# Product with v in float32: two heads in column halves, one broadcast per half later on, and an order planned with other durations

## The chip, the cores and the metric

One core of one Trainium2 chip. The metric is the device time of one execution in microseconds (us). The engines are TensorE (PE, with its weight loads shown apart as PEld), VectorE (DVE), ScalarE (ACT), GpSimd (POOL) and SyncE (SP), which issues most DMAs.

## The reference, cut to what matters

```python
def _attn_ref(q, k, v, g_norm):            # 8 batches, 8 heads, 576 x 64: linear attention
    kv = np.einsum('bhsd,bhse->bhde', k, v)
    out = np.einsum('bhsd,bhde->bhse', q, kv)
    rms = np.sqrt(np.mean(out * out, axis=-1, keepdims=True) + 1e-06)
    return (out / rms * g_norm).astype(np.float32)
...
def _moe_ref(x, w_gate, wq, wk, wv, wo):   # x: 8 x 576 x 512, 4 experts, the top 2 kept
    ...
    for e in range(E):
        q = x @ wq[e]
        k = x @ wk[e]
        v = x @ wv[e]
        scores = scale * (q @ k.transpose(0, 2, 1))
        scores = np.where(causal, -1000000000.0, scores)
        ...                                # softmax over the last axis: a
        ye = a @ v @ wo[e]
        ...                                # added where e is in the top 2, times its weight
def _moe2_ref(x, w_in, g_ln, w_sg, b_sg, w_out):
    h = gelu(x @ w_in)                     # 512 -> 1024, cut into u and v
    v_n = layer_norm(v) * g_ln
    v_s = np.einsum('ts,bsd->btd', w_sg, v_n) + b_sg[None, :, None]
    return x + (u * v_s) @ w_out
```

## The kernel before, in words

The work has two phases. Phase 1 goes over the 8 batches: `front` (k times v, q times that, the sum of squares), `normall` (the RMS scale), `qkpart` and `vpart` (projections for the four experts, called heads here), and `attn` (causal attention of the four heads, in five row blocks each: 128, 128, 128, 96, 96 rows). `conversions` splits the later weights into two parts in between. Phase 2 is the gated MLP, whose products the trace calls `ps`.

Most products run in the one-pass type float32r. To keep float32 accuracy an operand is split into a high part and the rest (`hi` and `lo`, or `h` and `l` at the end of a name), and the products of the parts are added up in PSUM. A product in plain float32 stands in the trace as two MATMUL rows per instruction of the program: `kvps` (k times v), `outps` (`outT`, q times that), `statps` (`stat`, four 32-column tiles side by side, marked by `together`) and `wxps`.

For a head e, `scores` makes the scores (`scps`), their masked minimum (DVE, into `prob` and `small`) and the exponential (ACT). `transp` transposes a row block on PE (`tps`), copies it as float32r into `aTh` (ACT), and writes the rest, `tps` minus `aTh`, into `aTl` (DVE). `av` multiplies with v: the tile `vst` holds, per head, 64 columns of v's high part and 64 of its rest, so a product gives both in 128 PSUM partitions (`avps`). It runs 7 pairs of products per head (over `aTh`, then `aTl`), with 256, 128, 320, 320, 320, 192 and 96 columns. ACT copies one half of `avps` to `avt`, DVE adds the other into `gav`. After the second head of a pair, the gate weights `R` are transposed (`rps`) and multiplied in, and `gav` is split and written to DRAM for phase 2.

`norm` broadcasts the scale `rr` over the partitions by a product with `bsel_sb`, into the tile `nps`, for two halves of 288 columns in each of 4 column groups. The loop `for _ in range(2)` issues that product twice.

The order on each engine is not that of the code. Every call is first recorded as an `Op`; `merge` interleaves the generators by the windows in `OPT["w"]` (in batches; `u` is the first part of phase 2), and `Recorder.plan` then plays the recorded operations through a model of the chip: `cost` gives each a duration, `LAG` the signalling time, `RATE` the DMA rate, `Clock` the TensorE clock. An engine takes the earliest recorded operation that is ready by the model and whose tiles are free. `trace` emits the program in that order, so the queue of each engine is fixed. Every instruction of it has the line of the call in `trace`, L440; the tile names tell them apart. Attention tiles in PSUM (`scps`, `tps`, `avps`, `rps`) share four banks, the other phase 1 tiles three, `statps` has one.

Of the kernel before, what the change touches and what calls it, by code (L numbers as in the profile page):

```python
# [48 lines left out]
OPT = dict(ob=1, sx=0, pinq=0, dv=0, pin=1, cvb=2, xb=1, ldb=2, hp={}, n1=0, n2=0, f1=0, pa=4, sA=(), dg=0, cost=(1.01, 0.88, 1.22, 1.47, 1.28), avi=1, prb=4, ahb=2, alb=2, qkb=2, ahead=3, w={'attn': (0.206, 1.26), 'qk1': (0.056, 0.272), 'qk0': (-0.534, -0.135), 'v': (-0.716, -0.324), 'front': (-1.368, -0.958), 'norm': (-0.947, -0.848), 'conv': (-0.324, 3.644), 'conv2': (3.213, 7.228), 'wts': (-1.719, -1.149), 'u': (0.212, 1.281), 'front_0': (-1.763, -1.646), 'v_0': (-1.24, -0.97), 'qk0_0': (-1.252, -1.036), 'qk1_0': (-0.092, 0.063), 'norm_0': (-1.641, -1.541)})  # L49
# [21 lines left out]
LAG = {"tensor": 0.25, "vector": 0.15, "scalar": 0.15, "gpsimd": 0.15, "sync": 0.6, "dma": 0.4}  # L71
RATE = 220e3
# [92 lines left out]
class Op:  # L165
    __slots__ = ("eng", "fn", "args", "kw", "tiles", "pred", "succ", "need", "n", "idx", "dur", "ready", "start", "done", "work", "group")
# [65 lines left out]
class Recorder:  # L232
# [16 lines left out]
    def together(self, ops):  # L249
        first = ops[0]  # L250
        for op in ops:
            op.group = ops
            first.pred.update(o for o in op.pred if o not in ops)
            first.need += [t for t in op.need if t not in first.need]

    def add(self, eng, fn, args, kw):
# [39 lines left out]
        op.dur = self.cost(op, outs, ins)  # L296
        if eng == "tensor":
            passes = 2 if fn == "transpose" else 4 if ins[0].dtype == F32 else 1
            op.work = min(op.dur, op.n * passes / 2400.0)
# [3 lines left out]
    def cost(self, op, outs, ins):  # L303

        n, fn = op.n, op.fn
        if op.eng == "tensor":
            if fn == "transpose":
                return 0.110
            if ins[0].dtype == F32 and len(outs[0].part) == 32:
                return n / 2400.0  # L310
            if ins[0].dtype == F32:
                return max(n * 4 / 2400.0, 0.22)
            return max(n / 2400.0 + 0.0125, 0.11)
        if op.eng == "vector":
            if fn == "memset":
                return 0.15
            extra = {"scalar_tensor_tensor": 0.06, "tensor_tensor_reduce": 0.09, "reciprocal": 0.05}.get(fn, 0.0)
            return 0.155 + 0.00103 * n + extra
        if op.eng == "scalar":
            return 0.155 + 0.00089 * n + (0.33 if "accum_out" in op.kw else 0.0) if fn != "preload_act_table_set" else 1.3  # L320
        if op.eng == "gpsimd":
            return 0.7 if fn == "dma_start" else max(0.5, 0.12 + 0.0023 * n)
        return 0.5

    def plan(self, margin=LAG):
# [30 lines left out]
        now, chain = 0.0, []  # L356
        while events:
# [11 lines left out]
            for e in self.ENGINES:  # L369
# [3 lines left out]
                for k, (_, op) in enumerate(row):  # L373
# [12 lines left out]
                    free_at[e] = now + op.dur  # L386
                    if e == "tensor":
                        free_at[e] += op.dur * sum([c.half(now) for c in clocks]) / len(clocks)
                        for c in clocks:
                            c.add(now, free_at[e], op.work)  # L390
                    push(free_at[e], "free", None)
                    end = free_at[e]
                    if op.fn == "dma_start":
                        size = self.size(op)
                        pipe = max(pipe, end) + size / RATE
                        end = pipe + 1.8
                    elif e == "tensor":
                        end += 0.1
                    op.done = end
                    push(end + 0.05, "gone", op)  # L400
                    for s in op.succ:
                        lag = 0.05 if s.eng == e and op.fn != "dma_start" else margin[s.eng]
                        if op.fn == "dma_start":
                            lag += margin["dma"]
                        if s.eng == e == "tensor":
                            lag = -0.1
                        s.ready = max(s.ready, end + lag)
# [41 lines left out]
class Phase1:  # L449
# [31 lines left out]
    def first_loads(self):  # L481

        nc = self.nc
        more = self.vv.tile([P, 2, 2, NQ, P], F32, name="kvmore", tag="vst")
# [14 lines left out]
    def staging(self, n):  # L499
        k = len(self.stg)  # L500
        return self.at.tile([P, n], F32, name="wstage", tag=f"aT{'hl'[k // 2]}1", bufs=2)
# [144 lines left out]
    def qk_half(self, st, pr, is_k, h):  # L646
        nc = self.nc
        col = 256 * is_k + P * pr
# [34 lines left out]
    def vproj(self, st, s):  # L683
        nc = self.nc
        m = _rows(s)
# [12 lines left out]
        nc.scalar.copy(vst[:m, s, :, 0:64], src)  # L698
        nc.vector.tensor_tensor(vst[:m, s, :, 64:128], src, vst[:m, s, :, 0:64].bitcast(F32), op=OP.subtract)
# [54 lines left out]
    def vpart(self, b, st):  # L754
        nc = self.nc
        st["qs"], st["kh"], st["kl"] = [], [], []
        st["vst"] = self.vv.tile([P, NQ, E, P], F32R, name="vst", tag="vst")
# [64 lines left out]
    def transp(self, st, e, i):  # L822
# [4 lines left out]
        if i == 0:  # L827
            st["aT"][e] = tuple(
                (
                    self.at.tile([P, 2, 256], F32R, name=f"aT{n}0", tag=f"aT{n}0", bufs=bf),  # L830
                    self.at.tile([P, NQ, 320], F32R, name=f"aT{n}1", tag=f"aT{n}1", bufs=bf),
                )
                for n, bf in (("h", OPT["ahb"]), ("l", OPT["alb"]))
            )
        hi, lo = st["aT"][e]
        ps = self.bank("tps", True)
        full = min(i + 1, 4)
        for j in range(i + 1):
# [3 lines left out]
        jobs = [  # L842
            (ps[:, 0 : full * m].rearrange("p (j f) -> p j f", j=full), lambda t: t[n][:, 0:full, q : q + m])
        ]
        if i == 4:
            jobs.append((ps[:96, 4 * m : 5 * m], lambda t: t[1][:96, 4, q : q + m]))
# [5 lines left out]
    def av(self, b, st, e):  # L852
        nc = self.nc
        parts = st["aT"].pop(e)
        vst = st["vst"]
        if e % 2 == 0:
            st["gav"] = self.at.tile([P, S], F32, name="gav", tag="gav", bufs=1)
        gav = st["gav"]
        dst = gav[0:64] if e % 2 == 0 else gav[64:128]
        t = self.at.tile([P, S], F32, name="avt", tag="avt", bufs=2)  # L860
        for n, (c0, c1, js) in enumerate(((0, 256, 2), (256, S, NQ))):
            ps = self.bank("avps", True)[:, 0 : c1 - c0]
            for j in range(js):
                kr = _rows(j)
                q0 = max(c0, _first(j))
                for x, a in enumerate(parts):
                    nc.tensor.matmul(
                        ps[:, q0 - c0 :],
                        vst[:kr, j, e, :],
                        a[n][:kr, j, q0 - c0 : c1 - c0],  # L870
                        start=(j == 0 and x == 0),
                        stop=(j == js - 1 and x == 1),
                    )
            nc.scalar.copy(t[64:128, c0:c1], ps[0:64])
            nc.vector.tensor_tensor(dst[:, c0:c1], ps[64:128], t[64:128, c0:c1], op=OP.add)
        if e % 2:
            R = st["R"][e // 2]
# [558 lines left out]
```

## Time and profile before

| | |
|---|---|
| median of 3 runs | 855.81 us (855.45 to 856.19) |
| profiled execution | 858.0 us, of which the span from first to last instruction is 856.2 us |
| granted TensorE clock | 0.992 of full, mean of the span |
| PE busy | 826.9 us (97%) |
| DVE, ACT, POOL busy | 526.0, 449.6, 321.9 us |

A matmul's busy time includes the time until its result is out, in which the next one already runs, so busy times of PE overlap. What a product takes of PE's time is the distance from its start to the start of the next one.

### The profile page before, as it was taken

What the parts mean: (1) busy time and instruction counts of PE and PEld (TensorE: products, weight loads), DVE (VectorE), ACT (ScalarE), POOL (GpSimd) and SP (SyncE); (2) the same over time, 40 slices, a digit from 0 to 9 for tenths busy, and PEclk for the clock granted to TensorE, in tenths of its full rate; (3) what the DMA queues carried; (4) which work ended last, traced back from release to release, by engine and by line L of the source; (5) the groups of instructions that cost most, each with busy time, mean ns of one, the idle gap of its engine ahead of it and who ended that gap; (6) DMA issues with size and microseconds to landing.
All of it is one profiled execution on the core that took longest, in us unless ns stands there. A gap on an engine that the chain in (4) does not pass through costs nothing.

```text
span 856.2 us, 16001 instructions
## 1 busy us (share of the span) xinstructions
PE 826.9 (97%) x5552; PEld 754.4 (88%) x5552; DVE 526.0 (61%) x1450; ACT 449.6 (53%) x1200; POOL 321.9 (38%) x387
## 2 busy tenths in 40 slices
PE   6599999999999999999998899999999999999998
PEld 5497999999899999998996789898989889898996
DVE  1657777887776776978886788453444435340330
ACT  2546566776766677676876794432333233321110
POOL 0872733854633253564651155231213222220120
PEclk9699999999999999999999999999999999999999
DMA  9576583874856768664549680111202030101011
GB/s 302 168 208 153 146 229 113 238 206 126 252 155 188 201 157 239 185 187 135 148 131 278 204 289 10 59 47 46 85 25 81 25 105 13 38 13 50 13 38 61
DMA packets 77090, 114.44 MB, mean 134 GB/s; under 512 B 13265, under 2 KB 40593, under 8 KB 77010
## 3 DMA queue, kind: packets, MB, share of 16 engines
q1 hardware_dynamic: 76866, 112.90, 45.1%
q8 instruction: 44, 0.72, 0.4%
q0 software_dynamic: 144, 0.52, 0.2%
q14 instruction: 36, 0.29, 0.1%
HBM read 58.31 MB, written 26.77 MB: 99 GB/s over the span
## 4 chain that ended last, share of the span: by engine, by line
PE 86%; DVE 5%; DMA 5%; ACT 1%; POOL 1%; issue 1%; SPq 1%; DVEq 0%; ACTq 0%
PE ps L440 42%; PE qkps L440 10%; PE scps L440 6%; PE vps L440 6%; PE avps L440 5%; PE tps L440 5%; PE kvps L440 3%; PE outps L440 3%; PE nps L440 2%; PE wxps L440 2%; DMA cv_w<-in_w_in 1%; DVE o L440 1%; DMA wstage<-in_wqkvg 1%; PE statps L440 1%; DMA kvmore<-in_kvp 1%; PE rps L440 1%
## 5 line engine op out<-in xcount | busy, mean ns | idle before, releaser
L440 PE MATMUL ps<-wsh,vn 128*128 128x288 f32 x576 | 120.2, 295 | 0.0
L440 ACT ACTIVATE prob<-prob,small 128x128 f32<-128x128 f32 (+4 forms) x160 | 96.8, 605 | 17.9 <-DVE small L440 16.3
L440 PEld LDWEIGHTS ps<-wsh,vn 128*128 128x128 f32 x576 | 94.3, 188 | 0.9 <-DVE g L440 0.3
L440 POOL TENSOR_TENSOR gl<-g,gh 128x512 fp32r<-128x512 f32 x32 | 41.6, 1300 | 135.5 <-ACT gh L440 135.4
L440 DVE CUSTOM_DVE_ANT_0 prob<-scps,mask_sb 128x128 f32<-128x128 f32 (+4 forms) x160 | 75.9, 478 | 25.9 <-PE scps L440 23.9
L440 DVE TENSOR_TENSOR aTl<-tps,aTh 128x384 fp32r<-128x384 f32 (+1 forms) x192 | 79.7, 432 | 6.2 <-ACT aTh L440 5.4
L440 PE MATMUL qkps<-xhi,whi 128*128 128x288 f32 x256 | 78.7, 307 | 0.0
L440 ACT CAST aTh<-tps 128x384 fp32r<-128x384 f32 (+1 forms) x192 | 69.1, 381 | 16.5 <-PE tps L440 14.4
L440 PE MATMUL qkps<-xhi,wlo 128*128 128x288 f32 x256 | 77.0, 301 | 0.0
L440 PE MATMUL qkps<-xlo,whi 128*128 128x288 f32 x256 | 77.0, 301 | 0.0
L440 PE MATMUL ps<-wsl,vn 128*128 128x288 f32 x256 | 75.5, 295 | 0.0
L440 PE MATMUL tps<-id_sb,prob 96*128 96x96 f32 (+2 forms) x480 | 71.7, 258 | 0.8 <-DVE small L440 0.4
L440 PE MATMUL scps<-kh,qs 128*128 128x128 f32 (+2 forms) x192 | 68.6, 361 | 2.0 <-DVE gav L440 0.6
L440 POOL TENSOR_SCALAR lny<-mv 128x1 f32<-128x1 f32 x36 | 24.3, 676 | 119.3 <-DVE mv L440 119.0
L440 ACT CAST gh<-g 128x512 fp32r<-128x512 f32 x32 | 19.9, 620 | 80.4 <-DVE g L440 62.8
L440 POOL TENSOR_TENSOR xlo<-o,xhi 128x576 fp32r<-128x576 f32 (+1 forms) x32 | 42.8, 1362 | 51.3 <-ACT xhi L440 51.2
L440 PE MATMUL avps<-aTh,vst 128*128 128x320 f32 (+4 forms) x224 | 59.0, 286 | 2.7 <-DVE gav L440 1.8
L440 DVE TENSOR_TENSOR g<-ps,u 128x288 f32<-128x288 f32 x64 | 28.9, 453 | 52.7 <-PE ps L440 52.7
L440 PE MATMUL scps<-kl,qs 128*128 128x128 f32 (+2 forms) x192 | 59.8, 315 | 0.4 <-DMA kl<-loT 0.4
L440 PEld LDWEIGHTS tps<-id_sb,prob 96*128 96x128 f32 (+2 forms) x480 | 52.8, 139 | 7.7 <-issue 2.8
L440 PE MATMUL avps<-aTl,vst 128*128 128x320 f32 (+4 forms) x224 | 56.4, 290 | 0.0
L440 ACT ACTIVATE vn<-vg,lny 128x512 fp32r<-128x512 f32 x32 | 22.9, 723 | 54.8 <-POOL lny L440 53.4
(177 smaller groups left out, 2431.7 us busy)
## 6 DMA issues: line engine op xcount, KB each, us to landing
kv<-in_kvp SPq DMA_DIRECT2D x30, 384.0 KB, 4.9
kh<-hiT SPq DMA_DIRECT2D x64, 144.0 KB, 3.0
kl<-loT SPq DMA_DIRECT2D x64, 144.0 KB, 3.1
q<-in_qT SPq DMA_DIRECT2D x30, 288.0 KB, 4.7
out<-oev SPq DMA_DIRECT2D x32, 256.0 KB, 2.0
kv<-in_kvp SPq DMA_DIRECT2D x30, 192.0 KB, 4.9
qs<-hiT SPq DMA_DIRECT2D x32, 144.0 KB, 2.6
qs<-loT SPq DMA_DIRECT2D x32, 144.0 KB, 2.6
```

The lines of the kernel that those rows point to most:

```text
L440: f(*[val(v) for v in op.args], **{k: val(v) for k, v in op.kw.items()})
```

## The change

The product with v takes plain float32: `aT` is one copy of the transposed block, in float32, made by ACT or DVE in turn; `vst` holds v once, 64 columns per head, also copied by ACT or DVE in turn. `av` now handles a pair of heads at once. The first head's 64 output rows go to PSUM partitions 0 to 63, the second's to 64 to 127, and the 14 products of the pair (28 MATMUL rows in the trace) are kept together in the order. One ACT copy per PSUM bank fills `gav`. In batches 1 to 7 the broadcast in `norm` is issued once. The planner's durations, lags and rate are other numbers, with a time for a change of tile size; the windows are other numbers as well. Three assertions state that the weights are recorded before use. The tile for two early loads no longer shares the buffers of `vst`.

```diff
@@ the windows (OPT) and the planner's numbers
-..., avi=1, prb=4, ahb=2, ..., w={'attn': (0.206, 1.26), ..., 'u': (0.212, 1.281), ...})
+..., avi=1, prb=4, ahb=4, ..., w={'attn': (0.177, 1.304), ..., 'u': (-0.111, 1.169), ...})
-LAG = {"tensor": 0.25, "vector": 0.15, "scalar": 0.15, "gpsimd": 0.15, "sync": 0.6, "dma": 0.4}
-RATE = 220e3
+LAG = {"tensor": 0.12, "vector": 0.13, "scalar": 0.13, "gpsimd": 0.13, "sync": 0.25, "dma": 0.12}
+MODE = 0.15
+RATE = 230e3
@@ def norm
-            for _ in range(2):
+            for _ in range(1 if b else 2):
                 nc.tensor.matmul(ps, self.bsel_sb[:, c, h, :], self.rr, start=True, stop=True)
@@ def vproj
-        nc.scalar.copy(vst[:m, s, :, 0:64], src)
-        nc.vector.tensor_tensor(vst[:m, s, :, 64:128], src, vst[:m, s, :, 0:64].bitcast(F32), op=OP.subtract)
+        (nc.scalar.copy if s % 2 else nc.vector.tensor_copy)(vst[:m, s], src)
@@ def transp
         for src, dst in jobs:
-            nc.scalar.copy(dst(hi), src)
-        for src, dst in jobs:
-            nc.vector.tensor_tensor(dst(lo), src, dst(hi).bitcast(F32), op=OP.subtract)
+            (nc.scalar.copy if (e + i) % 2 else nc.vector.tensor_copy)(dst, src)
@@ def av
+        for n, (c0, c1, js) in enumerate(parts2):
+            ps = banks[n]
             for j in range(js):
                 kr = _rows(j)
+                q0 = max(c0, _first(j)) - c0
+                ops += [
                     nc.tensor.matmul(
-                        ps[:, q0 - c0 :],
-                        vst[:kr, j, e, :],
-                        a[n][:kr, j, q0 - c0 : c1 - c0],
+                        ps[64 * h : 64 * h + 64, q0:],
+                        vst[:kr, j, 2 * pr + h, :],
+                        parts[h][n][:kr, j, q0 : c1 - c0],
...
+                    for h in range(2)
+                ]
+        nc.together(ops)
+        for ps, (c0, c1, _) in zip(banks, parts2):
+            nc.scalar.copy(gav[:, c0:c1], ps)
@@ def attn
-                if i == OPT["avi"] and e > 0:
-                    with self.hp("a"):
-                        self.av(b, st, e - 1)
-                    yield 1.0
-        self.av(b, st, E - 1)
-        yield 1.0
+                if i == OPT["avi"] and e == 2:
+                    self.av(b, st, 0)
+                    yield 2.0
+        self.av(b, st, 1)
+        yield 2.0
```

Three places of the order on PE follow. The first is the broadcast of batch 1, PE before (`kh`, `kl`, `qs` are the split k and q of batch 0's attention, which goes on meanwhile):

```order
L440 MATMUL nps<-rr,bsel_sb 128x288 x2
L440 MATMUL scps<-kh_576,qs_463 96x288
L440 MATMUL scps<-kl_587,qs_463 96x288
L440 MATMUL nps<-rr,bsel_sb 128x288 x2
L440 MATMUL scps<-kh_576,qs_463 96x288
L440 MATMUL scps<-kl_587,qs_463 96x288
```

PE now, at the same place:

```order
L453 MATMUL nps<-rr,bsel_sb 128x288
L453 MATMUL tps<-id_sb,prob 128x128
L453 MATMUL scps<-kh_564,qs_473 96x288
L453 MATMUL scps<-kl_572,qs_473 96x288
L453 MATMUL nps<-rr,bsel_sb 128x288
L453 MATMUL scps<-kh_564,qs_473 96x288
L453 MATMUL scps<-kl_572,qs_473 96x288
```

One broadcast per half stands where two stood; other products still lie between two halves.

The second place is the product with v of a head in the last batch, PE before, and ahead of it the transposes that fill the next head's tile:

```order
L440 MATMUL tps<-id_sb,prob 128x128 x2
L440 MATMUL avps<-aTh_7215,vst 128x256
L440 MATMUL avps<-aTl_7222,vst 128x256
L440 MATMUL avps<-aTh_7215,vst 128x128
L440 MATMUL avps<-aTl_7222,vst 128x128
L440 MATMUL avps<-aTh_7266,vst 128x320
L440 MATMUL avps<-aTl_7275,vst 128x320
```

PE now, the first pair of batch 1, with what stands ahead of it:

```order
L453 MATMUL tps<-id_sb,prob 128x128 x2
L453 MATMUL qkps<-xhi,whi 128x288
L453 MATMUL qkps<-xlo,whi 128x288
L453 MATMUL qkps<-xhi,wlo 128x288
L453 MATMUL qkps<-xhi,whi 128x288
L453 MATMUL qkps<-xlo,whi 128x288
L453 MATMUL qkps<-xhi,wlo 128x288
L453 MATMUL avps<-aT_1685,vst 64x256
L453 MATMUL avps<-aT_1830,vst 64x256
L453 MATMUL avps<-aT_1685,vst 64x128
L453 MATMUL avps<-aT_1830,vst 64x128
```

The two heads' tiles alternate, and 64 rows of output stand where 128 stood. In 13 of the 16 pairs projections (`qkps`, at times with two broadcasts behind them) stand in this way between the last transposes and the block, in the last pair seven of phase 2's first products; in the last pair of batch 6 and the first of batch 7 it is a few scores at most.

The third place is where phase 2 joins the last batch's attention, PE before. Between the last projection of batch 7 and the first `ps` row stand 28 `scps`, 26 `tps`, 28 `avps` and 5 `rps` products and nothing else:

```order
L440 MATMUL scps<-kh_7129,qs_7057 128x256
L440 MATMUL scps<-kl_7144,qs_7057 128x256
L440 MATMUL ps_7386<-wih_7280,xh 128x512
L440 MATMUL ps_7392<-wih_7280,xh 128x512
L440 MATMUL ps_7395<-wih_7280,xh 128x512
L440 MATMUL ps_7400<-wih_7280,xh 128x512
L440 MATMUL tps<-id_sb,prob 128x96 x4
```

PE now; between the last projection and the first `ps` row stand 34 `scps`, 38 `tps`, 28 `avps` (two pairs) and 5 `rps`:

```order
L453 MATMUL avps<-aT_6565,vst 64x96
L453 MATMUL avps<-aT_6678,vst 64x96
L453 MATMUL ps_6764<-wih_6643,xh 128x512
L453 MATMUL ps_6769<-wih_6643,xh 128x512
L453 MATMUL ps_6772<-wih_6643,xh 128x512
L453 MATMUL ps_6774<-wih_6643,xh 128x512
L453 MATMUL rps<-id_sb,R 128x128 x3
```

Behind the last scores and ahead of the first product that needs normalized rows (`ps<-wsh,vn`), 28 `ps` products of 512 columns now stand where 6 stood, and 60 of 288 columns in both.

## Rows read from the trace of the kernel before

**Rows 1.** The page: span, and busy time of each engine over the span.

```profile
span 856.2 us, 16001 instructions
PE 826.9 (97%) x5552; PEld 754.4 (88%) x5552; DVE 526.0 (61%) x1450; ACT 449.6 (53%) x1200; POOL 321.9 (38%) x387
```

**Rows 2.** Windows: from:to, length, busy per engine, granted clock, DMA share, GB/s.

```profile
0.00:50.00 50.00, 33.51 (x186) 29.23 (x187) 21.89 (x55) 19.58 (x53) 26.03 (x43) 0.86 0.74 224
50.00:400.00 350.00, 348.30 (x2675) 326.08 (x2673) 270.95 (x888) 245.18 (x722) 171.97 (x200) 1.00 0.67 186
400.00:447.00 47.00, 46.33 (x355) 44.12 (x355) 41.85 (x137) 33.95 (x102) 25.59 (x32) 1.00 0.48 131
447.00:500.00 53.00, 46.39 (x292) 37.97 (x290) 41.14 (x120) 39.14 (x102) 13.87 (x18) 1.00 0.71 222
500.00:856.00 356.00, 352.39 (x2053) 317.06 (x2051) 150.17 (x255) 111.71 (x226) 84.47 (x98) 1.00 0.17 57
```

**Rows 3.** Waits of PE, whole span: us in total, times, longest.

```profile
PE nps L440 <- DVE rr L440: 9.3, 1, 9.3
PE kvps L440 <- DMA kv<-in_kvp: 4.7, 2, 4.4
```

**Rows 4.** Timeline of PE, one head's product with v: start, us, what.

```profile
315.63 0.28 PE L440 MATMUL avps<-aTh,vst 128*128 128x256 f32 x1
...
317.18 0.23 PE L440 MATMUL avps<-aTh,vst 96*128 96x96 f32 x1
317.24 0.28 PE L440 MATMUL avps<-aTl,vst 96*128 96x96 f32 x1
317.35 0.32 PE L440 MATMUL vps<-whi,xhi 128*96 128x260 f32 x1
```

**Rows 5.** Timeline of PE around the four-tile float32 product of batch 3.

```profile
173.23 0.30 PE L440 MATMUL qkps<-xhi,whi 128*128 128x288 f32 x1
173.37 0.29 PE L440 MATMUL qkps<-xlo,whi 128*128 128x288 f32 x1
173.59 1.18 PE L440 MATMUL statps<-sq,sel_sb 128*32 128x288 f32 x16
174.70 0.44 PE L440 MATMUL tps<-id_sb,prob 128*128 128x128 f32 x2
```

**Rows 6.** The chain that ended last, a float32 product across the whole array: start, us.

```profile
65.52 0.97 PE outps L440 x4
```

**Rows 7.** Timeline of PE, broadcasts of a later batch.

```profile
294.53 0.44 PE L440 MATMUL nps<-rr,bsel_sb 128*128 128x288 f32 x2
294.80 0.28 PE L440 MATMUL avps<-aTl,vst 128*128 128x256 f32 x1
...
295.36 1.66 PE L440 MATMUL nps<-rr,bsel_sb 128*128 128x288 f32 x8
296.92 0.40 PE L440 MATMUL qkps<-xhi,whi 128*128 128x288 f32 x1
```

**Rows 8.** Groups on DVE and ACT: count, busy us, mean ns, idle before them.

```profile
L440 DVE TENSOR_TENSOR aTl<-tps,aTh 128x384 fp32r<-128x384 f32 (+1 forms) x192 | 79.7, 432 | 6.2 <-ACT aTh L440 5.4
...
L440 ACT CAST aTh<-tps 128x384 fp32r<-128x384 f32 (+1 forms) x192 | 69.1, 381 | 16.5 <-PE tps L440 14.4 <-DVE aTl L440 0.8
...
L440 DVE TENSOR_TENSOR gav<-avps,avt 64x256 f32<-64x256 f32 x64 | 29.1, 460 | 5.7 <-ACT avt L440 3.9
...
L440 ACT COPY avt<-avps 64x256 f32<-64x256 f32 x64 | 24.9, 392 | 8.7 <-PE avps L440 7.7
...
L440 DVE TENSOR_TENSOR vst<-vps,vst 128x256 fp32r<-128x256 f32 (+1 forms) x40 | 16.4, 415 | 0.7 <-ACT vst L440 0.7
```

**Rows 9.** The chain that ended last, where phase 2 begins: start, us, what.

```profile
447.45 0.57 DVE aTl L440
...
458.24 5.30 DMA xl<-gvl
...
486.95 1.25 ACT aTh L440 x3
488.20 0.04 issue
488.24 1.17 DVE aTl L440 x3
```

More of the change, by code (lines that the diff above doesn't have):

```diff
@@ L165 @@
 class Op:
-    __slots__ = ("eng", "fn", "args", "kw", "tiles", "pred", "succ", "need", "n", "idx", "dur", "ready", "start", "done", "work", "group")
+    __slots__ = ("eng", "fn", "args", "kw", "tiles", "pred", "succ", "need", "n", "idx", "dur", "ready", "start", "done", "work", "group", "lat", "load", "mode")
     def __init__(self, eng, fn, args, kw):
@@ L249, in together @@
     def together(self, ops):
-        first = ops[0]
+        first, tiles = ops[0], P // ops[0].mode[1]
         for op in ops:
-            op.group = ops
+            op.group, op.dur, op.load, op.work = ops, op.dur / tiles, op.load / tiles, op.work / tiles
+            op.lat = op.dur + 0.17
             first.pred.update(o for o in op.pred if o not in ops)
@@ L354, in can @@
             return True
-        now, chain = 0.0, []
+        now, chain, mode, last = 0.0, [], (P, P), 0.0
         while events:
@@ L385, in plan @@
                     op.start = now
-                    free_at[e] = now + op.dur
                     if e == "tensor":
-                        free_at[e] += op.dur * sum([c.half(now) for c in clocks]) / len(clocks)
-                        for c in clocks:
-                            c.add(now, free_at[e], op.work)
+                        half = sum([c.half(now) for c in clocks]) / len(clocks)
+                        turn = MODE if op.mode != mode else 0.0
+                        begin = max(now + turn, (now + turn if turn else last) + op.load)
@@ L391, in plan @@
+                        mode, last = op.mode, begin
+                        free_at[e] = begin + op.dur * (1 + half)
+                        for c in clocks:
+                            c.add(begin, free_at[e], op.work)
+                        end = free_at[e] + op.lat - op.dur
+                    else:
+                        free_at[e] = now + op.dur
+                        end = now + op.lat
                     push(free_at[e], "free", None)
-                    end = free_at[e]
                     if op.fn == "dma_start":
[L394 to L398, printed above, removed]
+                        pipe = max(pipe, end) + self.size(op) / RATE
+                        end = pipe + 1.7
@@ L483, in first_loads @@
         nc = self.nc
-        more = self.vv.tile([P, 2, 2, NQ, P], F32, name="kvmore", tag="vst")
+        more = self.at.tile([P, 2, 2, NQ, P], F32, name="kvmore", tag="more", bufs=1)
         for n in range(NC):
@@ L500, in staging @@
         k = len(self.stg)
[L501 removed]
+        return self.at.tile([P, n], F32, name="wstage", tag="aT1", bufs=OPT["ahb"])
     def load(self, n, kv=None, q=None):
@@ L827, in transp @@
         if i == 0:
[L828 to L835, printed above, removed]
+            st["aT"][e] = [
+                self.at.tile([P, 2, 256], F32, name="aT0", tag="aT0", bufs=OPT["ahb"]),
+                self.at.tile([P, NQ, 320], F32, name="aT1", tag="aT1", bufs=OPT["ahb"]),
+            ]
+        aT = st["aT"][e]
         ps = self.bank("tps", True)
@@ L849, in transp, with av @@
-        for src, dst in jobs:
-            nc.vector.tensor_tensor(dst(lo), src, dst(hi).bitcast(F32), op=OP.subtract)
-    def av(self, b, st, e):
+            (nc.scalar.copy if (e + i) % 2 else nc.vector.tensor_copy)(dst, src)
+    def av(self, b, st, pr):
         nc = self.nc
[L854 to L862, printed above, removed]
+        parts = [st["aT"].pop(2 * pr + h) for h in range(2)]
+        vst, R = st["vst"], st["R"][pr]
+        gav = self.at.tile([P, S], F32, name="gav", tag="gav", bufs=1)
+        parts2 = ((0, 256, 2), (256, S, NQ))
+        banks = [self.bank("avps", True)[:, 0 : c1 - c0] for c0, c1, _ in parts2]
+        ops = []
+        for n, (c0, c1, js) in enumerate(parts2):
+            ps = banks[n]
@@ L892, in attn @@
+        hi = self.at.tile([P, S], F32R, name="gvh", tag="gvh", bufs=1)
+        lo = self.at.tile([P, S], F32R, name="gvl", tag="gvl", bufs=1)
+        nc.scalar.copy(hi, gav)
+        nc.gpsimd.tensor_tensor(lo, gav, hi.bitcast(F32), op=OP.subtract)
+        for t, dst in zip((hi, lo), self.gvd[b]):
+            nc.sync.dma_start(dst[pr].bitcast(F32), t.bitcast(F32))
     def attn(self, b, st):
```

98 lines of the change are left out of this document (48 added, 50 removed).

## The prediction

> **What bounds the kernel now.** I read the page first: PE is busy for 826.9 of 856.2 us, DVE for 526.0, ACT for 449.6 [rows 1]. Then the windows, to see where that average hides something. From 50 to 400 us PE is busy for 348.3 of 350 us, from 500 on for 352.4 of 356, and the granted clock is 1.00 [rows 2]. In these stretches PE is the limit, and every microsecond of its work that goes shortens the span, unless something new becomes late. Two stretches differ. In the first 50 us PE is busy for 33.5 us; the waits name one of 9.3 us for `rr` and two for loads [rows 3]. From 447 to 500 us, where the last batch's attention has no projections left beside it and phase 2 begins, PE is busy for 46.4 of 53 us. That understates the gap, since busy times overlap. Weight loads show it better: in the dense stretch they are busy for 326.08/350 = 0.93 of the time, here for 37.97 us, which at 0.93 is 40.8 us of dense work, so some 12 us are lost (10.4 us by the density of 500 to 856 us, 0.89) [rows 2]. DVE is busy for 41.1 and ACT for 39.1 of the 53 us, and the chain runs from `aTh` on ACT to `aTl` on DVE and only then to the product with v [rows 2, 9].
>
> **The broadcast.** Seven batches times four groups times two halves are 56 products of 288 columns that go. Two adjacent ones with another product behind them take 0.27 us from start to start, 0.135 each, as the 0.14 of a projection of the same width [rows 5, 7]. So 56 x 0.135 = 7.6 us, in stretches where PE never rests. Bounds: eight in a row took 1.56 us to the next product, 0.195 each [rows 7], which gives 10.9 us. At the other end, that pace is set by who reads the banks, and then the second issue costs little: if PE had to wait for DVE anyway, 0. The new order puts scores and transposes between the halves in batch 1 and two broadcasts ahead of a block of 2.98 us (below) elsewhere, so DVE's reading is covered; I take 7.5.
>
> **The product with v.** A head's block now takes 317.35 - 315.63 = 1.72 us, 14 rows [rows 4]; 32 blocks are 55.0 us. The new block has, per head, 256 + 128 + 3 x 320 + 192 + 96 = 1632 columns in float32. What float32 costs on the whole array is seen at `outps`: four rows, two products of 288 columns, take 0.97 us, so 0.485 each or 1.68 ns per column [rows 6]. One head alone would take 1632 x 1.68 = 2.75 us, more than the 1.72 of two float32r passes. The change lives on two heads running side by side. No row of before has tiles of 64 columns, but `statps` has four of 32: 16 rows, eight float32 products of 288 columns. One after another these would take 8 x 0.485 = 3.88 us; the next product starts 1.11 us behind the first, where four abreast give 0.97. The remaining 0.14 us, and the 0.22 - 0.13 = 0.09 us longer step from the projection into the block, are the price of going to the other tile size and back [rows 5]. So a pair takes 2.75 + 0.23 = 2.98 us, sixteen take 47.7 us, and 7.3 us go.
>
> Weights: each half loads 64 columns per pass. The 96-column product whose next weights are not ready yet takes 0.11 us where its neighbour takes 0.06 [rows 4]; if 128 columns of load cost 0.11 us and the two halves load in turn, only the 96-column step (0.08 us a pass at 0.84 ns) is short, by 0.03 us twice a pair: 1 us in all. Not abreast at all, a pair takes 2 x 2.75 + 0.23 = 5.73 us, sixteen 91.7 us: 36.7 us more than now. I take the gain of 7.3, since the nearest row shows four abreast without loss.
>
> A block must not wait for the last copy of its second head. In 13 pairs six or more projections (0.8 us at 0.13) lie between the last transposes and the block, in the last pair phase 2's products; a copy takes 0.38 to 0.43 us [rows 8]. Two pairs have little cover: at most about 0.5 us each, 1 us.
>
> **Copies.** DVE loses `aTl` (79.7 us), the `gav` sums (29.1) and the rest of v (16.4), and gains 96 of the copies that ACT made at 0.38 us and 24 copies of v at 0.42 or less: -125 + 37 + 10 = -78 us. ACT loses half of its 69.1 us of `aTh`, and `avt` (24.9), and gains 32 copies of `gav` at about 0.39: some -47 us, more with the copies of v that it gives up [rows 8]. Beside a full PE this is worth nothing; that work was hidden. It counts where PE waits, from 447 to 500 us: there the two-step `aTh` then `aTl` becomes one step, and DVE, some 78% busy, loses about a fifth of the 376 us that it works up to 500 us [rows 2]. Also, 28 wide products of phase 2 instead of 6 now stand behind the last scores, 22 x 0.23 = 5 us of work that lies beside the first normalizations (0.23 is 512 columns at 0.13/288 a column). Against it, the stretch ahead has three heads without filler where it had two and some. Bounds: 0, and the whole 10 to 12 us. I take half, 6 us; the load of `xl` (5.3 us in the chain [rows 9]) and the normalization stay.
>
> **The rest.** The first 50 us keep both issues, the loads come in nearly the same order and `rr` hangs on the same steps of DVE and ACT: 0, with 1.5 us either way. The planner's new numbers move rows within a stretch; between 50 and 400 and after 500 us an order can't make PE's work shorter, so 0 there, with a loss of up to 5 us if shorter lags place a product ahead of its data.
>
> **Sum.** 7.5 + 7.3 + 6 = 20.8 us from the span's 856.2 give 835.4. The profiled execution took 858.0 us, 1.8 more than its span, and the median of the runs (855.81) lies 0.4 us below that span; I let that stand: 835 us.
>
> **The rivals.** *The halves run one after the other* (slower). Then the product with v costs 36.7 more instead of 7.3 less: 855.8 + 36.7 - 7.5 - 6 = 879 us. It decides once the pair takes more than (55.0 + 13.5)/16 = 4.28 us, that is once less than about half of one head's time is hidden behind the other. For it: no 64-column tile is seen, and the weights are twice as wide as those of `statps`. Against it: the row of four abreast. 4%.
>
> *Partly abreast.* Two streams and two weight loads get in each other's way, and the pair takes 3.2 to 4.2 us: with 3.7 us it is 59.2 us, 4.2 more than now, and the time is 846 to 847. For it speaks only the width. The Trainium skill's page "TensorE: Matmul & The Clock Gate", "Measured speedup vs the span model", gives three column tiles a speedup of 2.38; two at that efficiency would make 1.59 instead of 2 (an estimate from that page), 5.5/1.59 + 0.23 = 3.7 us a pair and the same 846 us. No row here shows such a loss: `statps` reaches 3.88/1.11 = 3.5 of 4 with the change of mode included. 7%.
>
> *The work goes but waits take its place.* The order was planned with shorter lags; products come to the head of PE's queue before their data, and 447 to 500 us stays as it is: 14.8 us less work, 3 to 12 us of new waits, 844 to 853 us. For it: PE's queue can't pass a late product. Against it: the middle has long runs of projections as cover. 8%; and 2% that such waits exceed 17 us, so slower.
>
> *The broadcasts and blocks were not the limit* (the change does not do what it says): another engine paces 50 to 400 us, and the time stays within 0.2% (1.7 us; I call less no change). PE busy for 348 of 350 us speaks against it. 2%.
>
> *All of the tail comes back, and the broadcasts are worth their upper bound*: 855.8 - 10.9 - 7.3 - 12 = 825.6, so 824 to 828 us. 4%.
>
> **How the numbers follow.** The forecast, 835 us with a range of its own from 828 to 843, has 73%; with the cases above this is 100%. 827 to 848 us leaves out the serial halves (4%), the slower waits and the unchanged case (4%), the top half of the other waits (4%) and half of the best case (2%), 14%. Faster: 73 + 7 + 8 + 4 = 92%; same 2%; slower 4 + 2 = 6%.
>
> **What would show it.** Right: `avps` has 448 rows, in sets of two that start within some 0.02 us; a pair takes 2.9 to 3.1 us from its first row to the next product; `nps` has 72 rows; DVE's busy time falls to about 450 us and ACT's to about 400; the weight-load density from the last projection to the solid `ps` run rises and that stretch shortens by some 6 us; phase 2's solid run stays at about 336 to 356 us. Wrong: the second half of a set starts 0.2 to 0.5 us behind the first; waits of PE for `aT` at the head of the blocks or a granted clock under 1.00 in the middle; or the long wait for `rr` grown past 11 us.

## The result, and the profile after

The changed kernel takes 847.24 us (median of 4 runs, 846.26 to 848.11), the kernel before 855.80 beside it: a ratio of 0.990 (95% interval 0.9882 to 0.9917). It is faster, by 8.6 us, where 20.8 were forecast; the time lies inside the range, near its upper end. The page of the profiled execution (847.4 us, to be read beside [rows 1]):

```profile
span 845.6 us, 15457 instructions
PE 811.3 (96%) x5496; PEld 722.2 (85%) x5496; DVE 462.3 (55%) x1274; ACT 398.0 (47%) x1048; POOL 321.9 (38%) x387
```

PE lost 15.6 us of busy time, DVE 64 and ACT 52; the prediction had 400 us for ACT and 450 for DVE, which is busy for 12 us more than that. The windows, with the columns of [rows 2] (the fourth row is the tail, as the fourth of [rows 2], some 10 us earlier):

```profile
0.00:50.00 50.00, 33.94 (x172) 28.02 (x173) 21.51 (x54) 19.04 (x52) 28.39 (x45) 0.83 0.75 224
50.00:400.00 350.00, 343.27 (x2682) 306.56 (x2681) 237.36 (x785) 213.48 (x629) 188.19 (x219) 1.00 0.70 191
400.00:437.00 37.00, 37.00 (x304) 35.12 (x303) 24.08 (x95) 22.23 (x65) 10.01 (x12) 1.00 0.49 129
437.00:488.00 51.00, 43.27 (x283) 34.04 (x282) 32.54 (x95) 31.50 (x79) 15.15 (x19) 0.93 0.67 209
488.00:845.00 357.00, 353.78 (x2065) 318.44 (x2064) 146.85 (x248) 111.80 (x226) 80.11 (x93) 1.00 0.17 59
```

Between 50 and 400 us PE was busy for 348.30 of 350; now it is for 343.27. And in the tail the mean granted clock is 0.93, where it was 1.00. The waits of PE, whole span (us in total, times, longest), say where:

```profile
PE outps L453 <- DVE bd L453: 7.9, 3, 6.6
PE ps L453 <- ACT vg L453: 6.8, 1, 6.8
PE kvps L453 <- DMA kv<-in_kvp: 4.1, 1, 4.1
PE tps L453 <- ACT aT L453: 2.6, 4, 0.7
PE scps L453 <- DVE aT L453: 2.1, 3, 0.9
```

The first is the idle time ahead of `rr` under another name [rows 3]: `outps` of batch 1 now stands ahead of the broadcast. The second, 6.8 us in one piece, is new. The last two are new too: six of these seven waits end 1.8 to 2.4 us behind the start of a long `ya`, of which more below.

The product with v itself does what was forecast. PE around the first pair of batch 1:

```profile
103.51 0.29 PE L453 MATMUL qkps<-xhi,whi 128*128 128x288 f32 x1
103.73 2.98 PE L453 MATMUL avps<-aT,vst 128*64 128x256 f32 x28
106.64 0.45 PE L453 MATMUL statps<-sq,sel_sb 128*32 128x288 f32 x4
```

From the first row of the block to the next product it is 106.64 - 103.73 = 2.91 us, and 2.91 in 15 of the 16 pairs (2.98 forecast; two heads took 2 x 1.72 = 3.44 [rows 4]). The second row of a set starts 6 to 7 ns behind the first.

Where PE's time went, worked out from the timelines of PE as the distance from each product's start to the next one's, summed by the tile it writes (us; a wait counts to the product ahead of it). The last three columns are experiments:

| tile | before | after | `a_late` | `a_mid` | `a_best` |
|---|---|---|---|---|---|
| `avps` | 57.2 | 46.9 | 46.5 | 46.9 | 46.7 |
| `nps` | 23.7 | 18.2 | 18.2 | 19.4 | 19.4 |
| `scps`, `tps` | 116.0 | 112.0 | 111.9 | 108.7 | 108.6 |
| `qkps`, `vps` | 169.6 | 173.7 | 173.7 | 171.8 | 172.5 |
| `ps` | 371.7 | 379.2 | 371.9 | 379.3 | 372.6 |
| the others | 109.4 | 107.3 | 107.3 | 107.2 | 106.1 |
| sum | 847.7 | 837.3 | 829.5 | 833.2 | 825.8 |

The two products that the change is about lost 10.3 + 5.5 = 15.8 us; 14.8 were forecast. All else was to lose 6 more, and gained 5.5.

### The profile page after: what moved, and what is told of

The parts are those of the page before. It is cut to its first block, busy times and chain, and to the rows that moved or that the text cites. A ratio compares the mean times of both kernels' runs of the same rounds, so it can differ in the third digit from the quotient of the medians.

```text
span 845.6 us, 15457 instructions
## 1 busy us (share of the span) xinstructions
PE 811.3 (96%) x5496; PEld 722.2 (85%) x5496; DVE 462.3 (55%) x1274; ACT 398.0 (47%) x1048; POOL 321.9 (38%) x387
## 4 chain that ended last, share of the span: by engine, by line
PE 84%; DVE 7%; POOL 3%; ACT 3%; issue 2%; DMA 1%; SPq 0%; ACTq 0%; POOLq 0%; DVEq 0%
PE ps L453 42%; PE qkps L453 10%; PE vps L453 7%; PE scps L453 5%; PE tps L453 4%; PE avps L453 4%; PE kvps L453 4%; PE outps L453 4%; PE wxps L453 2%; PE nps L453 1%; DVE ya L453 1%; DVE yb L453 1%; DVE prob L453 1%; DMA q<-in_qT 1%; PE statps L453 1%
## 5 line engine op out<-in xcount | busy, mean ns | idle before, releaser
L453 DVE CUSTOM_DVE_ANT_0 prob<-scps,mask_sb 128x128 f32<-128x128 f32 (+4 forms) x160 | 73.8, 474 | 6.1 <-PE scps L453 5.3
L453 PEld LDWEIGHTS qkps<-xhi,whi 128*128 128x128 f32 x256 | 48.7, 190 | 2.4 <-issue 1.7
L453 PE MATMUL ps<-wo2h,gl 128*128 128x512 f32 x128 | 50.1, 391 | 0.0
L453 PE MATMUL ps<-wo2l,gh 128*128 128x512 f32 x128 | 50.0, 391 | 0.0
L453 PE MATMUL ps<-wo2h,gh 128*128 128x512 f32 x128 | 49.9, 390 | 0.0
L453 PEld LDWEIGHTS qkps<-xlo,whi 128*128 128x128 f32 x256 | 48.9, 191 | 0.4
```

Of the source, the lines that this page charges most:

```text
L453: f(*[val(v) for v in op.args], **{k: val(v) for k, v in op.kw.items()})
```

## Two places in the trace where the rest was lost

**The tail.** PE, ACT and the windows (columns of [rows 2]) around the wait of 6.8 us:

```profile
475.86 0.29 PE L453 MATMUL ps<-xl,wih 128*128 128x288 f32 x1
482.95 0.61 PE L453 MATMUL ps<-xh,wih 128*128 128x288 f32 x1 [6.80 <-ACT vg L453]
483.35 0.44 PE L453 MATMUL ps<-xl,wih 128*128 128x288 f32 x1
```

```profile
476.77 0.63 ACT L453 ACTIVATE vg<-vraw 128x512 f32<-128x512 f32 x1 [0.65 <-DVE vn L453]
480.70 0.72 ACT L453 ACTIVATE vn<-vg,lny 128x512 fp32r<-128x512 f32 x1 [3.30 <-POOL lny L453]
482.30 0.60 ACT L453 ACTIVATE vg<-ps 128x512 f32<-128x512 f32 x1 [0.88 <-DVE vn L453]
```

```profile
476.00:480.40 4.40, 0.15 (x2) 0.00 (x0) 3.81 (x7) 0.76 (x2) 2.33 (x4) 1.00 0.00 0
480.40:483.00 2.60, 0.05 (x1) 0.05 (x1) 0.82 (x2) 1.42 (x3) 0.26 (x1) 0.50 0.00 0
483.00:487.20 4.20, 4.15 (x16) 3.80 (x17) 2.23 (x5) 1.54 (x3) 2.65 (x3) 0.50 0.18 70
```

The 512-column products that make v of phase 2 hold a PSUM bank until ACT's Gelu (`vg`) has read it. Phase 2's first part (`ps1`) has four banks. The Gelu stands in ACT's queue behind `vn`, which waits for POOL's `lny`, and a `vg` buffer is free only after DVE's `vn`. So the next 288-column product, which needs no normalized row at all, finds no bank for 7 us. The granted clock, full (2.4 GHz) since 43.5 us, falls to its lower level (1.2 GHz) from 480.4 to 487.2 us, in this idle time. The products from 482.95 to 487.2 take 0.24 us each in place of 0.13, another 2 us.

**The middle.** The four engines around one of the waits in batch 3's attention:

```profile
222.20 1.42 POOL L453 TENSOR_TENSOR gvl<-gav,gvh 128x576 fp32r<-128x576 f32 x1 [5.32 <-ACT gvh L453]
```

```profile
222.41 1.53 DVE L453 SCALAR_TENSOR_TENSOR ya<-yb,ya 128x288 f32<-128x288 f32 x1
```

```profile
223.97 0.43 ACT L453 CAST yh<-ya 128x288 fp32r<-128x288 f32 x1 [0.95 <-DVE ya L453]
224.31 0.47 ACT L453 COPY aT<-tps 128x384 f32<-128x384 f32 x1
```

```profile
224.84 0.63 PE L453 MATMUL tps<-id_sb,prob 96*128 96x96 f32 x5 [0.75 <-ACT aT L453]
```

`ya` is a step of the RMS scale of the next batch. It starts 0.2 us behind POOL's `gvl` and ends 0.3 us behind its end. ACT's `yh` waits for it, a copy `aT` stands behind `yh`, and PE waits for the bank that this copy frees. How often that happens shows in the rows of the tile `ya` (ns, least, median, most), before and after:

```profile
L440 DVE SCALAR_TENSOR_TENSOR ya<-yb,ya x8: 452/460/861, 30.9 to 397.4; 128x288 f32<-128x288 f32 x8
```

```profile
L453 DVE SCALAR_TENSOR_TENSOR ya<-yb,ya x8: 459/1397/1531, 28.8 to 385.0; 128x288 f32<-128x288 f32 x8
...
L453 DVE SCALAR_TENSOR_TENSOR o<-o,g_sb,nps x64: 500/508/517, 31.9 to 401.7; 128x288 f32<-128x288 f32 x64
```

In the new order `ya` stands beside `gvl` in six of seven later batches, before in none. The last row is the control: `o` has the same form, but reads one operand from PSUM, and is never longer than 0.517 us, though 40 of the 64 run beside a POOL operation for 0.2 us or more. The Trainium skill's page "SBUF — State Buffer", "SBUF: two separate sides" (with its part "Who interferes with whom"), says that a DVE operation with two inputs in SBUF and a GpSimd operation that reads SBUF exclude each other for the whole instruction, and that one with at most one SBUF input does not contend, unless it runs in a mode that uses two ports. This trace agrees for these two, 1.40 against 0.46 us for `ya` and 0.51 throughout for `o`. One SBUF tensor is no assurance, though: `yc`, `ya` times a factor per partition, takes 0.36 us as a rule, and 1.06 and 1.32 us in the two batches of the experiment `a_mid` (below) where it runs beside `gvl`; which mode it runs in, no row shows.

```profile
L460 DVE TENSOR_SCALAR yc<-ya,side x8: 354/362/1318, 30.6 to 380.8; 128x288 f32<-128x288 f32 x8
```

## The experiments

They ran on other chips than the first comparison, on which the kernel before took 856.3 to 857.4 us; so ratios to it are compared (the changed kernel: 0.990). "In its own order" means that the planner saw the unchanged program, and only the emission differs.

**Broadcasts twice again, `a_twice`.**

```diff
-            f(*[val(v) for v in op.args], **{k: val(v) for k, v in op.kw.items()})
+            for _ in range(op.alt or 1):        # alt = 2 for nps of batches 1 to 7
+                f(*[val(v) for v in op.args], **{k: val(v) for k, v in op.kw.items()})
```

> The changed kernel in its own order, with every broadcast of batches 1 to 7 issued twice in a row again; nothing else moves. If the broadcasts were full work of PE, as the forecast has it, 56 x 0.135 = 7.5 us come back: 847.2 + 7.5 = 854.8 us. If PE had spare time around them in the new order (it now waits some 7 us in the middle), less comes back: 847 to 851 us.

853.17 us, 0.9956 (0.9942 to 0.9971). The difference from 0.990 is 0.0056, 4.8 us, and 5.5 us by the spans (851.1 and 845.6). On the timeline `nps` takes 25.6 us in place of 18.2, the full 7.4, and the stretch in which these broadcasts stand, from the first scores to the last projection, is 6.1 us longer. So in the new order the broadcast is real work, worth 4.8 to 6.1 us where 7.5 were forecast.

**Once in the old order, `b_once`, and in batches 2 to 6 only, `b_once26`.** The second product is left out when the program is emitted, in the order of before.

> The kernel before in its own order, with the second of the two broadcasts left out in batches 1 to 7; nothing else moves. By the forecast's price 56 x 0.135 = 7.5 us go: a ratio of 0.991, about 848.3 us. If some of the broadcasts stood where PE would have waited for DVE's reading anyway, less: 850 to 855.

856.31 us, 0.9989 (0.9974 to 1.0005): no difference that can be measured, and by the interval a gain of at most 2.2 us. In the old order the price was not there. How long PE's weight loads waited ahead of the broadcasts for DVE's `o`, which reads the bank of `nps`, in the kernel before and in this run (us, times, longest):

```profile
PEld nps L440 <- DVE o L440: 1.6, 5, 0.6
PEld nps L442 <- DVE o L442: 3.8, 14, 0.6
```

A bank of `nps` becomes free when DVE has read it. In batches 1 to 7 a single broadcast now takes 0.24 us to the next product (median), where a pair took 0.33, so `nps` loses 3.9 us on the timeline (23.7 to 19.8) and not 7.5. Windows around the broadcasts of batch 1, columns of [rows 2]:

```profile
74.00:80.00 6.00, 5.41 (x31) 4.04 (x31) 5.62 (x17) 4.81 (x13) 2.10 (x2) 1.00 0.46 111
80.00:82.00 2.00, 1.15 (x8) 0.75 (x8) 1.94 (x4) 1.15 (x3) 2.00 (x2) 1.00 0.19 66
82.00:85.50 3.50, 3.50 (x18) 3.50 (x19) 3.44 (x11) 1.17 (x3) 2.73 (x3) 0.51 0.11 37
```

From 74 to 80 us DVE is busy for 5.62 of 6 us. Behind the broadcasts, with PE busy for 1.15 of 2 us, the clock falls to half for 3.4 us; it does so again from 399.5 us on, behind the broadcasts of batch 7. These falls are no explanation of the missing gain, though. This execution has a mean granted clock of 0.986 over its span; ten of the twelve have 0.990 or more, so most probably did without such falls, and they took 854.5 to 858.0 us all the same. What eats the rest of the 3.9 us stays open.

> The kernel before in its own order, with the second broadcast left out in batches 2 to 6 only. With all seven left out the granted clock fell to half twice, for 3.4 us each, behind the broadcasts of batch 1 and of batch 7. If the missing broadcasts of these two batches are the cause, the clock stays full from 50 us on and the time is 2 to 4 us lower than with all seven left out, though 16 products more are done: a ratio of 0.994 to 0.997. If the falls have another cause they stay, or come elsewhere: 0.999 or more.

855.52 us, 0.9989 (0.9973 to 1.0005). The profile shows the clock full from 36 us on, and a span of 852.7 us in place of 854.0 with 16 products more. That is one execution of each program. Their other executions have much the same mean clock (0.990 to 0.994 in all twelve of this run, 0.990 to 0.993 in ten of twelve of `b_once`) and the same ratio, so whether the missing broadcasts cause the falls, and what the falls cost, stays open.

**The two heads one after the other, `a_serial`.**

```diff
+        order[k:] = sorted(group, key=lambda o: o.alt) + rest    # alt = (head, place in the block)
```

> The changed kernel in its own order, but inside each block of the product with v the 7 products of the first head stand ahead of the 7 of the second, so that two halves of the array are never fed by neighbours. If neighbours in the two column halves run side by side, as the block of 2.91 us in the trace says (one head alone by the float32 price is 2.75), a block becomes about 5.6 us and 16 of them cost 43 us more: about 890 us. If the pace of the block is set by something else (weight loads, the copies), it stays near 847 us.

880.40 us, 1.0276 (1.0259 to 1.0293). The block of the same pair as above:

```profile
104.21 5.29 PE L458 MATMUL avps<-aT,vst 128*64 128x256 f32 x28
109.44 1.18 PE L458 MATMUL statps<-sq,sel_sb 128*32 128x288 f32 x16
```

It is 5.22 us in place of 2.91, a factor of 1.79; 16 x 2.31 = 37 us, of which 34 reach the span. Neighbours in the two column halves do run side by side, and only neighbours do.

**The new work with the old planner and the old windows, `newwork_oldnum`.** The bodies of `cost`, `plan` and `together`, `LAG`, `RATE` and the windows are those of before; a pair's products are entered at half of their float32 time.

> The new work (product with v in float32 and in column halves, one broadcast, the new copies) planned with the old planner's numbers and the old windows. Theory A, the new numbers place products ahead of their data and cost what is missing: the new work alone gives at least the 14.8 us counted for it, 841 us or less, and the waits for aT and vg are shorter. Theory B, the new work needs the new numbers: the old ones don't know a pair's block and the gain is smaller, 847 us or more.

857.91 us, 1.0007 (0.9992 to 1.0022): both pieces of saved work, and no gain. Theory A falls in this form. The profiled execution is the fastest of the twelve (854.21 us), with the highest mean clock (0.990, the others 0.982 to 0.988), so it shows less of the loss than the others had. Its waits of PE, the four largest, and the wait of weight loads ahead of the broadcasts for DVE:

```profile
PE nps L442 <- DVE rr L442: 8.1, 1, 8.1
PE ps L442 <- ACT vg L442: 5.8, 1, 5.8
PE kvps L442 <- DMA kv<-in_kvp: 5.7, 2, 4.5
PE outps L442 <- DVE bd L442: 3.1, 5, 0.8
PEld nps L442 <- DVE o L442: 7.1, 22, 0.6
```

The last row was 1.6 us in 5 waits in the kernel before. The wait for `vg` is here as well, so it doesn't come from the shorter lags: both sets of numbers make it, with the last scores at 465.1 us here, 463.4 in the changed kernel and 481.8 before. What both sets have in common is a rate for transfers of 220 or 230 GB/s. The changed kernel's transfers between 455 and 480 us (GB/s in 40 equal slices):

```profile
GB/s 413 406 392 307 251 288 195 147 365 409 406 406 409 409 409 380 398 240 213 247 202 270 325 374 390 384 404 184 54 18 0 0 0 0 0 0 0 0 0 0
```

**Without POOL's long operation, `a_nolow`.** `gvl` is computed for 8 of 576 columns.

> The changed kernel in its own order; POOL's subtraction that makes gvl is cut from 576 to 8 columns in all 16 pairs and the low part written to DRAM is a copy of the high part, so the output's low part is left out. Theory: in 6 of the 7 later batches DVE's ya (0.46 us alone) takes 1.3 to 1.5 us because POOL's gvl runs beside it, ACT's yh and the copies aT behind it come late, and PE waits 0.6 to 1.1 us for a bank. Then ya is back at about 0.46 us, the waits of PE for aT (4.7 us in all) go, and the time falls by 4 to 6 us to 841 to 843. Rival: the banks are late because ACT and DVE hold too many copies in a row; then ya may be short, but the waits for aT stay and the time is within 1 us of 847.

841.90 us, 0.9828 (0.9811 to 0.9845), 6.2 us less than the changed kernel by the ratios, 5.1 by the spans. `ya`, and PE's waits from 50 to 430 us, all of them:

```profile
L453 DVE SCALAR_TENSOR_TENSOR ya<-yb,ya x8: 440/452/809, 28.4 to 379.4; 128x288 f32<-128x288 f32 x8
```

```profile
PE scps L453 <- DVE gav L453: 1.0, 2, 0.7
PE tps L453 <- DVE small L453: 0.6, 2, 0.4
```

The waits for `aT`, 4.7 us, are gone with the long `ya`, and no engine's order has changed. The rival, too many copies in a row, falls.

**The planner told of the contention, `a_mid`.**

```diff
+        wide = fn.startswith("tensor_") or fn == "scalar_tensor_tensor"
+        op.port = wide and op.n > 8 and all(t.pool.kw.get("space") != PSUM for t in op.need)
...
+                        if e == "vector" and op.port and 60 <= now < 430:
+                            wait = max(0.0, port - now)
+                        free_at[e] = now + op.dur + wait
...
+                        if e == "gpsimd" and op.port:
+                            port = free_at[e]
```

> The changed kernel, planned with one rule more between 60 and 430 us of the plan: an operation of DVE that reads and writes SBUF alone, started while POOL runs a wide operation, ends only after POOL. No work is changed. Theory: the planner then puts other work of PE into the place of the late copies; the waits of PE for aT (2.6 + 2.1 us) fall to under 1.5 us and the time by 3 to 5 us, to 842 to 844. Rival: the late ya holds ACT and the copies in any order, and the waits only change their names: within 1.5 us of 847.

843.50 us, 0.9836 (0.9813 to 0.9859). PE's waits between 50 and 430 us:

```profile
PE tps L460 <- DVE aT L460: 0.6, 1, 0.6
PE qkps L460 <- POOL xlo L460: 0.3, 1, 0.3
```

The long `ya` is still there (median 1.0 us, most 1.54), but nothing that PE needs at once stands behind it. The work is the same; the order alone brought 5.5 us by the ratios, 3.9 by the spans (845.6 and 841.7) and 3.7 by the medians.

**The tail planned with a faster rate, `a_late`, and the rate alone, `a_late_rate`.**

```diff
-            d = ... 0.32 if n <= 8 else 0.1 + 0.0022 * n
+            d = ... 0.68 if n <= 8 else 0.1 + 0.0022 * n
-                        pipe = max(pipe, end) + self.size(op) / RATE
+                        pipe = max(pipe, end) + self.size(op) / (320e3 if 430 <= now < 1000000000.0 else RATE)
```

> The changed kernel, planned with two other numbers from 430 us of the plan on: 320 GB/s for transfers in place of 230 (the trace shows 350 to 410 in this stretch) and 0.68 us for POOL's small operations in place of 0.32 (the trace: 0.57 to 0.79). Up to there the order is the same. Theory: the order of the tail was made for transfers that come later than they do; products that need no normalization stand behind those that hold a bank until ACT's vg. With them in front the wait of 6.8 us for vg and the half clock behind it (some 2 us) go: ratio to the kernel before 0.979 to 0.981, about 838 to 840 us. Rival: the normalization itself sets the time (DVE needs some 2.4 us for each of its nine tiles), so the wait only moves to the first product with vn: 843 to 847 us.

840.07 us, 0.9797 (0.9774 to 0.982): 8.8 us less than the changed kernel by the ratios, 7.7 by the spans (845.6 and 837.9) and 7.2 by the medians. PE's two largest waits between 430 and 490 us:

```profile
PE ps L453 <- ACT vg L453: 0.6, 1, 0.6
PE scps L453 <- DVE small L453: 0.4, 1, 0.4
```

The clock stays full from 44 us on. From 469.7 us on 288-column products stand among the 512-column ones, so there is a bank for work that needs no normalization while the Gelus catch up. The rival, that DVE's normalization sets the time, falls: the first product with `vn` starts at 482.9 us, where it started at 492.5.

> As the changed kernel, planned with 320 GB/s in place of 230 from 430 us of the plan on; POOL's small operations stay at 0.32 us. If the transfers' rate alone made the tail's order, the wait for vg and the half clock go as with both numbers: a ratio of 0.979 to 0.982, about 840 us. If POOL's price matters, waits for vn or lny come in their place: 842 to 847.

841.00 us, 0.9819 (0.9801 to 0.9836), with 1.6 us of waits for `vg`: most of the gain is the rate (6.9 us of 8.8 by the ratios, 6.2 of 7.2 by the medians).

**Both, `a_best`; everything at once, `a_all`; and `gvl` on DVE, `a_best_gvl`.**

> The changed kernel, planned with the two corrections that paid: DVE's SBUF operations end after a wide operation of POOL (from 60 us of the plan on), and 320 GB/s and 0.68 us for POOL's small operations from 430 us on. The first 60 us are planned as in the changed kernel. If middle and tail are two losses that don't touch each other, their gains add: 7.2 (tail alone) and 3.7 us (middle alone) from 847.2 give 836.3, within 1.5 us. If the tail's order depends on how the middle ends, 839 us or more.

835.87 us (834.78 to 836.94), 0.9758 (0.9736 to 0.9779): the two gains add. The sum of the medians' gains was 836.3 us; by the spans it is 834.0, and the span is 834.2; by the ratios it is 0.9733, a little below the interval. It is faster than both kernels. Its windows in the middle and the tail, to be read beside those of after (343.27 of 350 and 43.27 of 51 us):

```profile
50.00:400.00 350.00, 348.51 (x2718) 311.06 (x2717) 236.51 (x799) 217.55 (x637) 188.62 (x215) 1.00 0.68 193
...
437.00:488.00 51.00, 48.36 (x327) 39.94 (x328) 34.52 (x97) 38.70 (x92) 14.30 (x19) 1.00 0.77 260
```

> The changed kernel, planned with all three corrections over the whole time: transfers at 320 GB/s, POOL's small operations 0.68 us, and DVE's SBUF operations ending after a wide operation of POOL. No work is changed. If the work was worth what the forecast says and only the order lost it, the sum of what is lost now comes back: some 5 us of the middle, 7 to 9 of the tail, 1 to 2 of the start: 831 to 836 us. If new waits come in their places: 840 us or more.

841.24 us, 0.9804 (0.978 to 0.9828): with the faster rate from the start of the plan, and the rule of `a_mid` in the first 60 us too, 5.4 us are lost again by the medians, 3.9 by the ratios. `nps` of batch 0 now starts at 28.55 us in place of 31.02, but waits:

```profile
PE nps L460 <- DVE o L460: 5.1, 7, 1.4
```

The first scores start at 60.2 us, 2.2 later than in the changed kernel. The rest lies between them and the last projection, 378.0 us where `a_best` has 373.1; which waits make it was not followed up.

> As the run beside it, and the subtraction that makes gvl is done by DVE in place of POOL, so POOL's longest operation can no longer stand beside ya. DVE gets 16 operations of some 0.66 us more, POOL loses 16 of 1.4. If the contention is what the planner could not order away, 1 to 2 us less than the run beside it; if its rule already did, the same within 1 us, or 1 us more for DVE's work.

840.07 us, 0.9811 (0.9789 to 0.9833): 4 us worse than the run beside it. `ya` is short now (median 0.45 us), but from the first scores to the last projection PE takes 374.5 us where `a_best` takes 373.1, so taking away the contention that was left there brought nothing. The rest is another order in the tail: the clock is half from 450.3 to 457.1 us, and PE waits 2.4 us for one of phase 2's weights.

## Why the prediction was too high a gain

**Right: the two pieces of work.** The pair's block is 2.91 us (2.98), both column halves run abreast, and rivals one and two fall. That the gain of 15.8 us on the timeline stands so near to 14.8 is in part luck. `avps` lost 10.3 us where 7.3 were forecast, because the blocks of before make 57.2 us in all and not 32 x 1.72 = 55.0. `nps` lost 8.5 us in batches 1 to 7 and gained 3.0 in batch 0. The estimate of 3.7 us a pair, which carried over what the Trainium skill's page "TensorE: Matmul & The Clock Gate", "Measured speedup vs the span model", gives for three column tiles, does not hold here: two tiles of 64 columns gain a factor of 1.79 on the serial order of `a_serial`.

**The step that failed: the tail.** The prediction had "28 wide products of phase 2 instead of 6 now stand behind the last scores ... work that lies beside the first normalizations", and gave half of 12 us, 6. From the last projection to the end it is 409.59 us before (446.63 to 856.22) and 409.90 after: nothing. The relief itself is real. The attention's products in this stretch are nearly the same (65 `tps`, 15 `rps`, 46 `scps` where 48 stood, three pairs where five heads stood), and took 33.5 us on the timeline before and 26.3 after, 7.2 us less. But `ps` takes 379.2 us there where it took 371.7, and with the tail reordered (`a_late`) it is 371.9 again and the stretch 402.10 us. So a wide product is cover only until four of them hold the banks. I counted them as work beside the normalization, and didn't ask what frees their banks: the Gelu, on the very engine that the normalization occupies. 7 us of wait and 2 us of half clock took the gain back.

**Also wrong: "an order can't make PE's work shorter, so 0 there, with a loss of up to 5 us".** The loss was in the text, as a bound, and it came. From the first scores to the last projection `avps` and `nps` take 18.3 us less than before, but the stretch shortened only from 389.65 to 377.69 us, by 12.0. Of the 6.3 us between, 4.5 are the six waits for `aT` behind a long `ya`, by `gvl` beside it; without the long `gvl` (`a_nolow`) the stretch is 371.95 us, and with the other order (`a_mid`) 373.04. The rival of "waits take its place" had the right sum (844 to 853 us), and it had the tail that stays as it is; for the middle it had the wrong mechanism: no lag was too short there, an operation was three times as long as any planner thought.

**The start was mis-sized: 0, with 1.5 us either way.** The first scores stand at 56.98 us before and 58.03 after, 1 us. But the same old start gave 54.77 and 55.23 in `b_once` and `b_once26`, whose programs are the same up to there: the profiled execution of before, 2.2 us over its median, lost those at its start. So the new start costs about 3 us. The 16 broadcasts of batch 0 take 7.68 us there where they took 4.66, with `outps` of batch 1, in one of the three banks, standing right ahead of them, and the clock is half until 43.5 us instead of 39.8; that the bank is the cause was not tested. With this start the three stretches give -12.0 (middle) + 0.3 (tail) + 3 (start) = -8.7, where 8.6 were measured. Of the 12.2 us that are missing from the forecast, the tail is 6.3, the start 3 and the middle 2.8.

**The broadcast's 7.5 depends on the order.** In the new order it measured 7.4 us on the timeline and 4.8 to 6.1 in the time, the span and the stretch (`a_twice`). In the old one it was 3.9 us on the timeline and at most 2.2 in time (`b_once`), near the lower bound. The row that priced it, 0.27 us a pair, was a cheap one: in batches 1 to 7 of the kernel before the median pair took 0.33. DVE's relief alone doesn't bring the price either: with the new work in the old numbers (`newwork_oldnum`) the 72 broadcasts took 23.8 us on the timeline, as much as the 128 before.

## What to carry to other kernels

When work is taken off a full engine, ask of each stage that gets shorter which buffers its new neighbours hold and who frees them; work that fills a gap must be able to leave its PSUM bank without the engine that makes the gap. A planned order is as good as its durations: look up the operations whose least and most differ by a factor of three, and the transfers that land far ahead of the plan, before turning to the lags. And price a removed instruction in the order in which it is removed: the same 56 broadcasts were worth some 5 us in one and at most 2 in the other.

## What the runs showed of the hardware

Two float32 products in the two column halves of PE start 6 to 7 ns apart and cost one (2.91 us a pair, 5.22 with the heads one after the other). A DVE operation with both inputs in SBUF takes 1.3 to 1.5 us in place of 0.46 beside a POOL operation of 1.4 us; the same form with an input in PSUM stays at 0.51. A scaling of a single SBUF tensor took 1.06 and 1.32 us in place of 0.36 beside it. With PE idle from 476 to 483 us the granted clock was half from 480.4 to 487.2 us, so products behind the wait took 0.24 us each in place of 0.13 for 4 us.
